# A retention layer feeding a bilinear FFN: groups 4 and 5 of the tokens go through the FFN as two blocks of 256 instead of one of 512, and one output step is placed elsewhere

## The chip, the cores and the metric

The kernel runs on one core of a Trainium2 chip. A core has a matrix engine (TensorE, PE in the profile, with its weight loads as PEld), a vector engine (VectorE, DVE), a scalar engine (ScalarE, ACT), a general engine (GpSimd, POOL), a queue that issues DMAs (SyncE, SP), and sixteen DMA engines that carry them out. Each engine works through its own list of instructions in order; the engines wait for each other through semaphores. Matmul results land in PSUM, a small memory of eight banks, and ACT or DVE must read them out before a bank can be used again.

The metric is the device time of one execution in microseconds. The time shown for a kernel is the median of its runs.

## The reference: what is computed

Eight sequences of 576 tokens, eight heads of 64 features. First a retention layer (attention without a softmax, with a decay per head), then a feed-forward block with two multiplied branches:

```python
scores = scale * np.matmul(q, k.transpose(0, 1, 3, 2))
gamma = 1.0 - 2.0 ** (-5.0 - np.arange(H, dtype=np.float32))
rel = pos[:, None] - pos[None, :]
Dmat = np.where(rel >= 0, gamma[:, None, None] ** rel[None, :, :], 0.0)
attn = np.matmul(scores * Dmat, v)              # (8, 8, 576, 64)
x = attn.transpose(0, 2, 1, 3).reshape(4608, 512)
out = ((x @ w_a) * (x @ w_b)) @ w_out           # 512 -> 1536 -> 512
```

The decay splits into a factor of the query's place and one of the key's place, so that a token's output is the sum of its own block of keys (masked scores) and a running state (the sum of key times value) over all blocks before.

## The kernel before, in words

**Groups.** The 4608 tokens are taken in 18 groups of 256, numbered from 0. Groups 0 to 2 go through an opening of their own. From group 3 on, a group is four pieces of 64 tokens, and its retention is done in small matmuls of 64x64, four of which share the array: `keyed` (L517) makes the pieces' key-value products in two PSUM tiles `kv0` and `kv1`; `matched` (L590) makes the scores of each piece with itself in `sc`; `open_outputs` (L659) starts the outputs `o` from the running states; `close_outputs` (L669) adds the masked scores times values. DVE then adds the products up to running sums (`add`, L555), ACT casts sums to states (`convert`, L567, and `convert_swapped`, L578), DVE scales outputs into the FFN's input `xT` (`scaled`, L647) and masks the scores (`masked`, L606).

**A stretch.** `stretch(into, outof)` (L679) issues these in one piece on PE: outputs of group `outof` from its states, products and scores of group `into`, outputs of `outof` from its keys. With `outof` None there are no outputs, and the products go into the PSUM buffer of `o`, which is free then; otherwise `kv0` and `kv1` are taken from the pool `ps_ffn`. `open_alone(n)` (L675) and a bare `close_outputs(n)` do a group's outputs without any scores. What DVE and ACT have to do after a stretch is put on a list, `later`, and taken off it one entry at a time by `pop` (L278) at fixed places of the FFN: the sums, the two scalings, then the first cast with the first masking, then the swapped casts with the second masking. `SPLIT` (L48) names the groups 3 and 5, whose four sums are two entries rather than one.

**The FFN.** `ffn_block` (L729) does one block of `n` tokens (`blocks`, L111: 512, 256, 256, then 512 each). For each of twelve columns F of 128 hidden features: four matmuls make `pa` (L747), ACT copies it to `ha` (L755), four make `pb` (L762), and DVE multiplies `ha` by `pb` into `hT` (L767). Each matmul streams the block's `n` tokens past a weight tile of 128x128, which is loaded for it. Then, for each 128 tokens, twelve matmuls make `po` (L781); it is copied out to `osb` by ACT (L790), or in blocks of 512 by ACT and DVE (L792) in turn, and stored by a DMA from SP. `pa`, `pb`, `po`, `kv0` and `kv1` all come from `ps_ffn`, a pool of four PSUM banks (L89). A bank can be handed on only when the reading of its tile has been issued; the choice is made when the program is built, and the new tile's first matmul waits for that reading.

**The order.** The whole order is written out by hand. The FFN's loop counts its matmuls in units of one 512-column matmul; a list `todo` (L916 to L948) holds steps with the count at which each is issued, and the FFN issues a due step at its next edge, which is the end of a `pb` or every fourth matmul of `po`. A block of 512 is 144 units (96 for `pa` and `pb`, 48 for `po`), one of 256 is 72 (48 and 24). The stretches around the change are due at 197, 240, 336, 372 and 408 units, the fifth group's outputs alone at 272 and 276. Also on the list are `ahead` (L461, POOL's casts of the loaded q, k, v), `turn` (L495, DMAs that transpose q and k into `qkT`, on SP) and `load_pair` (L140, the loads, on SP). SP issues loads, transposes and stores in the order in which the list and the FFN name them.

**The blocks and what falls in them.** Units 0 to 144 are groups 0 and 1, 144 to 216 group 2, 216 to 288 group 3, and 288 to 432 groups 4 and 5 in one block. A group's outputs must be scaled into `xT` before its block begins.

Of the kernel before, what the change touches and what calls it, by code (L numbers as in the profile page):

```python
# [18 lines left out]
def kernel(  # L19
# [15 lines left out]
    NTOK = B * S  # L35
# [72 lines left out]
    wb_sb = big.tile([128, NC, DFF], BF16)  # L108
    wo_sb = big.tile([128, NF, DM], BF16)

    blocks = [512, 256, 256] + [512] * ((NTOK - 1024) // 512)  # L111
    x_tiles = {}

    def x_of(t0, n):
# [797 lines left out]
    def turn_step(i):  # L912
# [9 lines left out]
    todo += [(136, total_of, (2,))]  # L922
    todo += [(28 + 6 * step, pair_tables, (step,)) for step in range(13)]
    todo += [(170, stretch, (3, None)), (197, stretch, (4, 3)),
             (240, stretch, (5, 4)), (272, open_alone, (5,)),
             (276, close_outputs, (5,)), (336, stretch, (6, None)),
             (372, stretch, (7, 6)), (408, stretch, (8, 7))]
    for n in range(8, NP, 2):
        todo += [(starts[n] - 116, stretch, (n + 1, n)),
# [61 lines left out]
```

## Time and profile before

| | us |
|---|---|
| median of 3 runs | 327.92 (327.43 to 328.18) |
| the profiled execution, its own time | 327.7 |
| its span, first to last instruction | 326.0 |
| PE busy | 315.8 (97%) |
| DVE busy | 161.6 (50%) |
| ACT busy | 129.5 (40%) |
| POOL busy | 116.4 (36%) |
| block of group 3, first `pa` to the next block's | 69.64 to 88.61 |
| block of groups 4 and 5 | 88.61 to 123.14 |

All durations further down are from the profiled execution; its granted clock was 1.000. A line of a timeline gives the start in us, the time until the last of the merged instructions ended, the engine, the source line, the operation with what it writes and reads, partitions and sizes, how many were merged (xN), and in brackets the idle time of the engine ahead of it with what ended that. Matmuls are pipelined: four of 256 columns are shown with 0.60 us, but the next four start 0.44 us after them. So the cost of a group of matmuls is read from start to start. A few matmul records can be missing.

### The profile page before, as it was taken

What the parts mean: (1) busy time and instruction counts of PE and PEld (TensorE: products, weight loads), DVE (VectorE), ACT (ScalarE), POOL (GpSimd) and SP (SyncE); (2) the same over time, 40 slices, a digit from 0 to 9 for tenths busy, and PEclk for the clock granted to TensorE, in tenths of its full rate; (3) what the DMA queues carried; (4) which work ended last, traced back from release to release, by engine and by line L of the source; (5) the groups of instructions that cost most, each with busy time, mean ns of one, the idle gap of its engine ahead of it and who ended that gap; (6) DMA issues with size and microseconds to landing.
All of it is one profiled execution on the core that took longest, in us unless ns stands there. A gap on an engine that the chain in (4) does not pass through costs nothing.

```text
span 326.0 us, 8627 instructions
## 1 busy us (share of the span) xinstructions
PE 315.8 (97%) x3576; PEld 165.3 (51%) x3615; DVE 161.6 (50%) x289; ACT 129.5 (40%) x286; POOL 116.4 (36%) x150
## 2 busy tenths in 40 slices
PE   8899999999999999999999999999999999999995
PEld 3564458768544554545454545454445444444443
DVE  5844454766437663845374626561556245314421
ACT  6844754453435524523253324442333233213321
POOL 3990068650867091747075205450520000000000
DMA  7999999999999989996899169925840500031013
GB/s 215 254 185 207 256 233 219 205 204 195 227 210 230 210 200 201 204 228 145 189 207 185 43 166 200 214 66 146 194 81 28 140 31 0 2 97 32 3 28 100
DMA packets 143175, 50.37 MB, mean 155 GB/s; under 512 B 124576, under 2 KB 138656, under 8 KB 143136
## 3 DMA queue, kind: packets, MB, share of 16 engines
q1 hardware_dynamic: 138384, 45.10, 66.5%
q0 software_dynamic: 4752, 4.72, 8.9%
q8 instruction: 28, 0.46, 0.6%
q14 instruction: 11, 0.09, 0.1%
HBM read 37.75 MB, written 9.44 MB: 145 GB/s over the span
## 4 chain that ended last, share of the span: by engine, by line
PE 92%; SPq 2%; DMA 2%; issue 1%; ACT 1%; DVE 1%; ACTq 0%; DVEq 0%
PE pb L762 29%; PE po L781 29%; PE pa L747 27%; SPq L159 2%; DMA qf<-in_q_dram 2%; PE o L626 2%; PE o L639 2%; PE sc L598 1%; PE kv L536 1%; PE pa L724 1%; DVE sT L350 0%; PE o L426 0%; PE sc L342 0%; PE tp L327 0%; PE tp L491 0%
## 5 line engine op out<-in xcount | busy, mean ns | idle before, releaser
L767 DVE TENSOR_TENSOR hT<-ha,pb 128x512 bf16<-128x512 bf16 (+1 forms) x120 | 75.7, 632 | 98.1 <-PE pb L762 89.9
L755 ACT CAST ha<-pa 128x512 bf16<-128x512 f32 (+1 forms) x120 | 64.7, 543 | 119.8 <-PE pa L747 115.5
L762 PE MATMUL pb<-xT,wb_sb 128*128 128x512 bf16 (+1 forms) x474 | 111.2, 358 | 0.7 <-ACT osb L790 0.2
L747 PE MATMUL pa<-xT,wa_sb 128*128 128x512 bf16 (+1 forms) x452 | 106.8, 356 | 1.4 <-issue 1.0
L781 PE MATMUL po<-wo_sb,hT 128*128 128x512 bf16 (+2 forms) x429 | 94.8, 373 | 1.7 <-issue 1.4
L762 PEld LDWEIGHTS <-wb_sb 128*128 128x128 bf16 x480 | 46.9, 98 | 47.0 <-issue 0.7
L747 PEld LDWEIGHTS <-wa_sb 128*128 128x128 bf16 x468 | 44.9, 98 | 44.3 <-issue 0.2
L781 PEld LDWEIGHTS <-hT 128*128 128x128 bf16 x444 | 41.8, 98 | 47.2
L468 POOL CAST qkb<-qf 64x1024 bf16<-64x1024 f32 x15 | 15.5, 1030 | 74.0 <-DMA qf<-in_q_dram 74.0
L473 POOL TENSOR_TENSOR vb<-vf,vs 128x1024 bf16<-128x1024 f32 x15 | 28.5, 1901 | 11.9 <-DMA vf<-in_v_dram 7.3
L792 DVE COPY osb<-po 128x512 f32<-128x512 f32 (+1 forms) x16 | 10.9, 682 | 39.7 <-PE po L781 39.7
L790 ACT COPY osb<-po 128x512 f32<-128x512 f32 (+1 forms) x21 | 12.0, 570 | 45.2 <-PE po L781 44.7
L649 DVE TENSOR_TENSOR xT<-o,qs 128x512 bf16<-128x512 f32 x30 | 19.5, 682 | 5.2 <-PE o L639 5.2
L468 POOL CAST qkb<-kf 64x1024 bf16<-64x1024 f32 x15 | 15.7, 1047 | 12.3 <-DMA kf<-in_k_dram 11.7
L561 DVE TENSOR_TENSOR sums<-kv,sums 128x256 f32<-128x256 f32 x44 | 18.6, 423 | 2.8 <-PE kv L536 0.8
L607 DVE TENSOR_TENSOR sT<-sc,mask 128x512 bf16<-128x512 f32 x30 | 19.5, 679 | 0.0
L472 POOL CAST qkb<-kf 64x512 bf16<-64x512 f32 x30 | 17.6, 614 | 0.9
L472 POOL CAST qkb<-qf 64x512 bf16<-64x512 f32 x30 | 17.6, 614 | 0.6
L565 ACT CAST states<-sums 64x512 bf16<-64x512 f32 x26 | 16.0, 616 | 0.3
L310 POOL CAST qkb<-kf 128x512 bf16<-128x512 f32 x5 | 3.1, 614 | 16.5 <-DMA kf<-in_k_dram 16.5
L666 ACT COPY fence<-o 128x2 f32<-128x2 f32 x15 | 2.4, 161 | 16.2 <-PE o L626 16.2
L350 DVE TENSOR_TENSOR sT<-sc,mask_s 128x1024 bf16<-128x1024 f32 x6 | 7.3, 1221 | 2.5 <-PE sc L342 2.5
(87 smaller groups left out, 163.0 us busy)
## 6 DMA issues: line engine op xcount, KB each, us to landing
qf<-in_q_dram SPq DMA_DIRECT2D x32, 256.0 KB, 4.8
kf<-in_k_dram SPq DMA_DIRECT2D x32, 256.0 KB, 5.1
vf<-in_v_dram SPq DMA_DIRECT2D x32, 256.0 KB, 5.1
out_dram<-osb SPq DMA_DIRECT2D x25, 256.0 KB, 2.3
out_dram<-osb SPq DMA_DIRECT2D x20, 128.0 KB, 2.7
wo_sb<-in_moe_w_out_dram POOLq DMA_DIRECT2D x3, 512.0 KB, 16.0
qf<-in_q_dram SPq DMA_DIRECT2D x8, 128.0 KB, 3.3
kf<-in_k_dram SPq DMA_DIRECT2D x8, 128.0 KB, 3.4
```

Of the source, the lines that this page charges most:

```text
L468: nc.gpsimd.tensor_copy(qkb[0:64, w], t[0:64])
L472: nc.gpsimd.tensor_copy(to[:, :, 1 - r], fro[:, :, r])
L473: nc.gpsimd.tensor_tensor(vb.rearrange("p (k h d) -> p k h d", k=2, h=H), vf.rearrange("p (k h d) -> p k h d", k=2, h=H), vs2[:, 2 if n in ...
L561: nc.vector.tensor_tensor(sums[:, i], own, prev, op=ALU.add)
L565: nc.scalar.copy(to(half(1 - r)), fro(half(r)))
L607: nc.vector.tensor_tensor(sT[:, on].rearrange("p c k s -> p (c k) s"), sc[:, on].rearrange("p c k s -> p (c k) s"), mask3.unsqueeze(1).to_ ...
L649: nc.vector.tensor_tensor(x_of(t0, 128).rearrange("p c (a s) -> p c a s", a=2), o[:, :, :, kp].rearrange("p a c s -> p c a s"), qs[:, :, s ...
L747: nc.tensor.matmul(pa[:, 0:n], wa_sb[:, c, fs], xT[:, c], start=(c == 0), stop=(c == NC - 1))
L755: nc.scalar.copy(ha[:, 0:n], pa[:, 0:n])
L762: nc.tensor.matmul(pb[:, 0:n], wb_sb[:, c, fs], xT[:, c], start=(c == 0), stop=(c == NC - 1))
L767: nc.vector.tensor_tensor(hT[:, F, 0:n], has[F][:, 0:n], pb[:, 0:n], op=ALU.mult)
L781: nc.tensor.matmul(po[:, 0:width], hT[:, F, u * 128:(u + 1) * 128], wo_sb[:, F, cols], start=(F == 0), stop=(F == NF - 1))
```

## The change

The block of groups 4 and 5 becomes two blocks of 256. So group 5's outputs are needed 72 units later, at 360 instead of 288: its outputs alone (at 272 and 276) go away, and the stretch at 336, which had only group 6's products and scores, now has group 5's outputs as well. The stretch of group 5's scores with group 4's outputs moves from 240 to 256 units.

```diff
-    blocks = [512, 256, 256] + [512] * ((NTOK - 1024) // 512)
+    blocks = [512] + [256] * 4 + [512] * ((NTOK - 1536) // 512)
...
     todo += [(170, stretch, (3, None)), (197, stretch, (4, 3)),
-             (240, stretch, (5, 4)), (272, open_alone, (5,)),
-             (276, close_outputs, (5,)), (336, stretch, (6, None)),
+             (256, stretch, (5, 4)), (336, stretch, (6, 5)),
              (372, stretch, (7, 6)), (408, stretch, (8, 7))]
```

All other due times stay. In units, the two new blocks are 288 to 360 and 360 to 432, and everything from 432 on is the same list of steps as before.

## The prediction

> **What bounds the kernel now.** I read the page's busy times and its chain of waits first, then the timelines of PE, ACT and DVE from 64 to 124 us, since the change touches nothing before the block of group 3 and nothing after 432 units.
>
> From the page:
>
> ```profile
> span 326.0 us, 8627 instructions
> ...
> PE 315.8 (97%) x3576; PEld 165.3 (51%) x3615; DVE 161.6 (50%) x289; ACT 129.5 (40%) x286; POOL 116.4 (36%) x150
> ...
> PE 92%; SPq 2%; DMA 2%; issue 1%; ACT 1%; DVE 1%; ACTq 0%; DVEq 0%
> ```
>
> PE is the bound: it works 97% of the span and carries 92% of the chain. ACT and DVE are half idle as a mean, but the chain has 1% of each, and that 1% is all in the 256 blocks. PE's timeline in the block of group 3:
>
> ```profile
> 71.34 0.60 PE L762 MATMUL pb<-xT,wb_sb 128*128 128x256 bf16 x4 [0.23 <-ACT osb L790]
> ...
> 72.64 0.60 PE L747 MATMUL pa<-xT,wa_sb 128*128 128x256 bf16 x4
> 73.08 0.60 PE L762 MATMUL pb<-xT,wb_sb 128*128 128x256 bf16 x4
> 73.52 0.60 PE L747 MATMUL pa<-xT,wa_sb 128*128 128x256 bf16 x4
> ...
> 76.61 0.61 PE L747 MATMUL pa<-xT,wa_sb 128*128 128x256 bf16 x4
> 77.06 0.60 PE L762 MATMUL pb<-xT,wb_sb 128*128 128x256 bf16 x4
> 77.68 0.60 PE L747 MATMUL pa<-xT,wa_sb 128*128 128x256 bf16 x4
> 78.24 0.60 PE L762 MATMUL pb<-xT,wb_sb 128*128 128x256 bf16 x4
> 78.74 0.60 PE L747 MATMUL pa<-xT,wa_sb 128*128 128x256 bf16 x4
> 79.42 0.60 PE L762 MATMUL pb<-xT,wb_sb 128*128 128x256 bf16 x4
> 79.85 0.60 PE L747 MATMUL pa<-xT,wa_sb 128*128 128x256 bf16 x4
> ```
>
> Undisturbed, a `pa` or `pb` of 256 columns takes 0.44 us from start to start (72.64, 73.08, 73.52), 109.4 ns a matmul. After the stretch that ends at 76.61 the starts are 0.45, 0.62, 0.56, 0.50, 0.68, 0.43 apart: three columns take 3.24 us instead of 2.625, a stall of 0.615 us. The reason is the banks: `kv0` and `kv1` hold two of four until DVE has added them up, so each `pa` waits for ACT's copy of the last, each `pb` for DVE's product. DVE in the same stretch:
>
> ```profile
> 77.76 0.42 DVE L767 TENSOR_TENSOR hT<-ha,pb 128x256 bf16<-128x256 bf16 x1 [1.81 <-PE pb L762]
> 78.10 0.42 DVE L561 TENSOR_TENSOR sums<-kv,own 128x256 f32<-128x256 f32 x1
> 78.55 0.42 DVE L561 TENSOR_TENSOR sums<-kv,sums 128x256 f32<-128x256 f32 x1
> 78.94 0.42 DVE L767 TENSOR_TENSOR hT<-ha,pb 128x256 bf16<-128x256 bf16 x1
> ```
>
> Here group 5 is one of the two whose sums are split, so only two (0.45 us apart) stand ahead of the next product. ACT before the stall of 71.34:
>
> ```profile
> 67.86 0.41 ACT L568 CAST states<-sums 128x256 bf16<-128x256 f32 x1
> 68.27 1.24 ACT L565 CAST states<-sums 64x512 bf16<-64x512 f32 x2
> 69.53 0.82 ACT L565 CAST left_states<-sums 64x256 bf16<-64x256 f32 x2
> 70.70 0.58 ACT L790 COPY osb<-po 128x512 f32<-128x512 f32 x1 [0.35 <-PE pb L762]
> ```
>
> An odd batch's second half has four swapped casts, 2.06 us of ACT in a row; in a `po` phase they cost PE 0.39 us (71.34 instead of 70.95). In blocks of 512 a column lasts 1.73 us, and there is no such stall: 96 + 48 matmuls of 216 ns (93.80 to 95.52 is eight) are 31.1 us, and with the stretches below that is the block's 34.5 us to 0.03.
>
> **The change part by part**, on PE unless another engine is named.
>
> (1) *Half the columns per matmul.* In `pa` and `pb` 96 matmuls of 512 become 192 of 256: 192 x 109.4 ns = 21.00 against 96 x 216 = 20.74. **+0.26 us.** `po` stays at 48 matmuls of 512.
>
> The Trainium skill ("TensorE: Matmul & The Clock Gate", section "Back-to-back issue gap") speaks harder against the change: in a real stream of weight loads and matmuls it gives some 81 ns a matmul at 128 columns and 131 at 512. Read straight between them, 256 would take 98 ns (an estimate from that page), two of them 65 ns more than one of 512, and this step would cost 6.2 us. The rows above, 109.4 and 216, decide: the page's 131 is not met anywhere in this trace.
>
> (2) *Stretches put together.* A full stretch costs 1.33 us: the `pb` started at 107.49 would hand over at 108.355, and the next `pa` starts at 109.69 (its `pb` at 110.55 less four matmuls). Group 6's stretch without outputs: 98.975 to 99.71, 0.735. Group 5's outputs alone: the `po` phase from 82.47 to 88.61 lasts 6.14 less 24 x 216 ns, 0.96. So 0.96 + 0.735 go and 1.33 comes. **-0.36 us.** The stretch lands on the last `pb`, so a `po` phase of 5.2 us follows: DVE's four sums (1.8), scalings (1.3) and masks (1.3) fit, ACT's two plain casts (0.8) and two swapped (1.24) end just before the second `osb` copy. No stall taken; without that cover it would be the 0.39 of (4) in the block of group 3.
>
> (3) *Group 5's scores at 256 instead of 240 units.* Two columns follow instead of three. Of the 0.615 us, the first five starts remain (0.18 + 0.12 + 0.06, the fifth tile now being `po`); the sixth, 0.24, goes. 0.615 - 0.37: **-0.24 us.**
>
> (4) *Group 7's scores at 372 units.* They fell into a block of 512 without a stall; now they fall behind the third column of a block of 256, with all that makes stalls there: group 7 is not split, and it is an odd batch's second half. With T for the start of the next `pa`, and the lags of the timeline above: `pa` T, T+1.07, T+2.13; `pb` T+0.45, T+1.63; DVE's first product at T+1.15, then all four sums at T+1.49 to T+3.26. The third `pb` gets `kv0`'s bank, free after the third sum at T+2.81, and starts at T+2.86 instead of T+2.19: 0.67 us. DVE then gives products 0.94 us apart (80.12, 81.06, 81.99 before) against PE's 0.875; one `pb` is 0.09 late. Then ACT: `ha` of column 7 is done at about T+5.2, the four swapped casts fill ACT until T+7.2, `ha` of column 8 until T+7.6. In the order of the built kernel, `pa` of column 10 reuses the bank of column 8's: it can start at T+7.67 instead of T+6.89, 0.78. Together **+1.54 us**. Below, nothing (if casts and sums are hidden as in the 512 blocks); above, 0.67 plus all 2.06 of ACT, 2.7. I take the middle, because the same queues in the block of group 3 gave 0.615 and 0.39.
>
> (5) *ACT and DVE work.* 24 `ha` of 373 ns replace 12 of 585 (ACT +1.9 us), 24 products of 418 replace 12 of 686 (DVE +1.8), two `osb` copies go from DVE (690) to ACT (586). Hidden under PE except where (4) counts them.
>
> (6) *SP and POOL.* The order of SP is unchanged up to group 7's transposes; then one store of the new block stands ahead of group 8's. Group 7's were issued at 101.0 and 103.2 and the second landed 3.8 us later, at 107.0; SP issues without a break before them, so they do not come earlier. Group 7's scores were at 109.0; now block 2 (of group 3) ends at 69.64 + 15.68 + 0.39 + 1.33 + 0.37 = 87.4, block 3 at 104.4, and the stretch starts at 107.05, its scores 0.65 later at 107.7. Margin 0.7 us: 0 taken, up to +1 if SP is slower. The added store waits for an `osb` of about 103.3, when SP still issues transposes, and takes 0.4 to 0.8; group 8's transposes land near 111, its scores come at 118. POOL's values of group 8 now wait for group 5's outputs at 99, and POOL needed them at 104: nothing.
>
> Sum: 0.26 - 0.36 - 0.24 + 1.54 = **+1.2 us**. The profiled execution took 327.7, 0.2 under the median; it would be 328.9, and the median 327.92 + 1.2 = 329.1. Everything from 432 units on moves by the same amount.
>
> **The rivals.**
>
> *R1, not slower: the four banks cover ACT's burst.* The mechanism is (4)'s last term: after column 7 PE can run two columns ahead (1.75 us) if both products have been made. If so the 0.78 goes, and the sum is +0.42; with the sums hidden too (as if `kv0` and `kv1` came free early) it is 0.26 - 0.36 - 0.24 = -0.34. It decides where ACT's hold-up stays under about 1.3 us; against it stands its length, 2.06. 327.6 to 328.4.
>
> *R2, group 7's transposes land late.* SP's transposes took 1.25 to 2.6 us to issue and 3.1 to 5.2 to land; 1 or 2 us more than above and PE stands in front of the scores, 0.3 to 1.3 us, on top of (4). Against it: the order ahead is unchanged and SP does not wait for PE there. 329.4 to 330.4.
>
> *R3, the stall at 372 feeds itself.* A late `pb` delays DVE, whose masks delay the scores of group 8 at 408 (one `sc` buffer), and ACT's late `ha` reaches into that stretch, whose outputs wait for ACT's fence copy. Up to the 2.7 of (4): 330.3.
>
> **How the numbers follow.** 0.2% of 328 is 0.66 us, about what a measurement of this kernel can tell from no change. My case, +0.7 to +1.9: 0.60. R2, to +2.5: 0.10. R3, +1.9 to +2.7: 0.08. R1: 0.22, of which 0.18 within 0.2% and 0.04 below. Slower is 0.78. The range leaves out R1's lower half and the top of R2 and R3: 328.2 to 330.5.
>
> **What would show it.** Right: from 69.64 to the block at 432 units 54.7 us instead of 53.5; `pa` and `pb` of 256 at 0.44 us in the new blocks; one piece of 1.33 us at the end of the first new block and none before it; behind group 7's stretch a `pa` that waits 0.6 to 0.9 us for ACT `ha`, and a weight load or `pb` that waits for DVE `sums`. Wrong: these waits under 0.5 us in all (R1), a wait of PE `sc` for the DMA of `qkT` (R2), waits at the stretch of group 8 (R3), or a difference that arises after 124 us, of which nothing here tells.

## The result, and the profile after

The median went from 328.05 us (327.43 to 329.16, six runs) to 329.59 us (329.38 to 330.74, six runs). The ratio is 1.0051, with a 95% interval of 1.0038 to 1.0064: the change makes the kernel slower by half a per cent, 1.5 us. The profiled execution took 329.72 us, its span is 328.0, its mean granted clock 0.998.

From the page of the changed kernel:

```profile
span 328.0 us, 8900 instructions
...
PE 319.9 (98%) x3711; PEld 174.7 (53%) x3711; DVE 162.3 (49%) x299; ACT 132.4 (40%) x300; POOL 116.6 (36%) x150
...
q8 instruction: 29, 0.48, 0.6%
...
PE 92%; SPq 2%; DMA 2%; ACT 1%; DVE 1%; issue 1%; ACTq 0%; DVEq 0%
...
L747 PE MATMUL pa<-xT,wa_sb 128*128 128x512 bf16 (+1 forms) x516 | 110.9, 340 | 0.9 <-ACT ha L755 0.9
```

PE's share of the span rose from 97% to 98% and its busy time by 4.1 us. The busy time alone would mislead. The trace of the kernel before lacks records, 3576 matmuls against 3615 weight loads, and shows fifteen idle gaps of 0.16 us that end with "issue", 2.4 us in all; the trace of the changed kernel has 3711 of each and no such gap. And a group of four matmuls is drawn 0.16 us longer than the step to the next one, so every wait is drawn that much too short. What is to be read is the length of the blocks, from the first `pa` of one to the first `pa` of the next:

| from, to | before | after |
|---|---|---|
| opening, up to the block of group 3 | 69.64 | 70.24 |
| block of group 3 | 18.98 | 17.47 |
| of it, waiting for `osb` | 0.39 | 0.08 |
| blocks of groups 4 and 5 | 34.52 | 17.02 + 20.41 |
| from 432 units to the end | 202.86 | 202.88 |

Lengths are worked out from unrounded starts and can differ by 0.01 from those of the printed ones. After 432 units nothing changed, to 0.02 us. The 0.60 us of the opening arose before any edit, and the wait for `osb` differs from execution to execution where the code is the same (0 to 2.2 us in the table below; 2.15 us of ACT's idle time there end with the landing of a store in e10). Without these two, the block of group 3 lost 1.21 us and the new blocks cost 2.91: +1.70 us in the profile, against +1.54 in the medians and +1.2 in the prediction.

The block of group 4 has nothing in it but its matmuls and one full stretch: 96 x 109.4 ns + 24 x 216 ns + 1.33 = 17.02 us, and it lasts 17.02. The block of group 5 has two full stretches, so it should last 18.35. It lasts 20.41, and the 2.07 us over lie in the stretch of group 7 (0.11) and behind it. PE's timeline there:

```profile
108.79 0.61 PE L747 MATMUL pa<-xT,wa_sb 128*128 128x256 bf16 x4
109.23 0.60 PE L762 MATMUL pb<-xT,wb_sb 128*128 128x256 bf16 x4
110.04 0.61 PE L747 MATMUL pa<-xT,wa_sb 128*128 128x256 bf16 x4 [0.20 <-ACT ha L755]
110.78 0.60 PE L762 MATMUL pb<-xT,wb_sb 128*128 128x256 bf16 x4
111.22 0.60 PE L747 MATMUL pa<-xT,wa_sb 128*128 128x256 bf16 x4
112.04 0.61 PE L762 MATMUL pb<-xT,wb_sb 128*128 128x256 bf16 x4 [0.22 <-DVE sums L561]
112.49 0.60 PE L747 MATMUL pa<-xT,wa_sb 128*128 128x256 bf16 x4
...
115.61 0.60 PE L762 MATMUL pb<-xT,wb_sb 128*128 128x256 bf16 x4
116.85 0.60 PE L747 MATMUL pa<-xT,wa_sb 128*128 128x256 bf16 x4 [0.65 <-ACT ha L755]
```

An undisturbed group starts 0.44 us after the one before. From 108.79 to 112.49 there are six steps from start to start, 2.62 us in all if nothing waited, and they take 3.70: 1.07 us of stall. Then 1.24 us pass between 115.61 and 116.85, a stall of 0.80, with 0.07 more just ahead of it. The brackets name only 0.20, 0.22 and 0.65: the idle time that the view shows is less than what is lost, because the four overlapping matmuls of a group are drawn 0.60 us long. DVE and ACT at the same place:

```profile
107.61 0.42 DVE L767 TENSOR_TENSOR hT<-ha,pb 128x256 bf16<-128x256 bf16 x1 [0.45 <-ACT ha L755]
110.31 0.42 DVE L767 TENSOR_TENSOR hT<-ha,pb 128x256 bf16<-128x256 bf16 x1 [2.28 <-PE pb L762]
110.65 1.79 DVE L561 TENSOR_TENSOR sums<-kv,sums 128x256 f32<-128x256 f32 x4
```

```profile
114.45 1.25 ACT L565 CAST states<-sums 64x512 bf16<-64x512 f32 x2
115.72 0.82 ACT L565 CAST left_states<-sums 64x256 bf16<-64x256 f32 x2
116.44 0.63 ACT L755 CAST ha<-pa 128x256 bf16<-128x256 f32 x2
```

DVE's first product behind the stretch starts 1.52 us after the first `pa` (110.31 - 108.79), where the prediction had 1.15, and the four sums follow it. The third `pb` (112.04) waits for the third sum. ACT's four swapped casts run from 114.45 to 116.54, and the `pa` of 116.85 waits for the copy of a column that is queued behind them.

### The profile page after: what moved, and what is told of

Its sections match the earlier page's. It is cut to its first block, busy times and chain, and to the rows that moved or that the text cites. A ratio compares the mean times of both kernels' runs of the same rounds, so it can differ in the third digit from the quotient of the medians.

```text
span 328.0 us, 8900 instructions
## 1 busy us (share of the span) xinstructions
PE 319.9 (98%) x3711; PEld 174.7 (53%) x3711; DVE 162.3 (49%) x299; ACT 132.4 (40%) x300; POOL 116.6 (36%) x150
## 4 chain that ended last, share of the span: by engine, by line
PE 92%; SPq 2%; DMA 2%; ACT 1%; DVE 1%; issue 1%; ACTq 0%; DVEq 0%
PE po L781 29%; PE pb L762 28%; PE pa L747 28%; SPq L159 2%; DMA qf<-in_q_dram 2%; PE o L626 2%; PE o L639 1%; PE sc L598 1%; PE kv L536 1%; PE pa L724 1%; DVE sT L350 0%; DVE sums L561 0%; PE o L426 0%; ACT states L565 0%; PE sc L342 0%
## 5 line engine op out<-in xcount | busy, mean ns | idle before, releaser
L767 DVE TENSOR_TENSOR hT<-ha,pb 128x512 bf16<-128x512 bf16 (+1 forms) x132 | 77.6, 590 | 104.5 <-PE pb L762 89.0
L755 ACT CAST ha<-pa 128x512 bf16<-128x512 f32 (+1 forms) x132 | 66.6, 508 | 118.0 <-PE pa L747 115.4
L762 PE MATMUL pb<-xT,wb_sb 128*128 128x512 bf16 (+1 forms) x528 | 113.6, 340 | 0.4 <-DVE sums L561 0.2
L747 PE MATMUL pa<-xT,wa_sb 128*128 128x512 bf16 (+1 forms) x516 | 110.9, 340 | 0.9 <-ACT ha L755 0.9
L781 PE MATMUL po<-wo_sb,hT 128*128 128x512 bf16 (+2 forms) x444 | 97.1, 374 | 0.0
L762 PEld LDWEIGHTS <-wb_sb 128*128 128x128 bf16 x528 | 51.6, 98 | 42.7 <-DVE sums L561 0.5
L747 PEld LDWEIGHTS <-wa_sb 128*128 128x128 bf16 x516 | 49.6, 98 | 41.7 <-issue 1.5
L790 ACT COPY osb<-po 128x512 f32<-128x512 f32 (+1 forms) x23 | 13.1, 571 | 46.3 <-PE po L781 46.3
L792 DVE COPY osb<-po 128x512 f32<-128x512 f32 (+1 forms) x14 | 9.5, 682 | 36.0 <-PE po L781 36.0
L808 PE MATMUL w<-ones 128*128 128x512 bf16 x19 | 7.1, 495 | 1.5 <-DVE idxp_f L203 1.5
```

Of the source, the lines that this page charges most:

```text
L747: nc.tensor.matmul(pa[:, 0:n], wa_sb[:, c, fs], xT[:, c], start=(c == 0), stop=(c == NC - 1))
L755: nc.scalar.copy(ha[:, 0:n], pa[:, 0:n])
L762: nc.tensor.matmul(pb[:, 0:n], wb_sb[:, c, fs], xT[:, c], start=(c == 0), stop=(c == NC - 1))
L767: nc.vector.tensor_tensor(hT[:, F, 0:n], has[F][:, 0:n], pb[:, 0:n], op=ALU.mult)
L781: nc.tensor.matmul(po[:, 0:width], hT[:, F, u * 128:(u + 1) * 128], wo_sb[:, F, cols], start=(F == 0), stop=(F == NF - 1))
```

## The experiments

The experiments' own times scatter by 1 to 4 us even for the kernel before (327.1 to 331.5 in the same sessions): in their profiles the block of group 3 began anywhere from 69.5 to 72.5 us, and its wait for `osb` was 0 to 2.2 us, mostly in kernels whose edit lies behind that. So a ratio of 0.3% says little here, and the readings rest on the lengths of the blocks in the profiles, one execution of each kernel. Column "3" is the block of group 3 without its wait for `osb`; columns "4" and "5" are the two new blocks (one of 512 in the kernel before).

| kernel | 3 | 4 | 5 | sum | median, and ratio to before |
|---|---|---|---|---|---|
| before | 18.59 | 34.52 together | | 53.11 | |
| after | 17.38 | 17.02 | 20.41 | 54.81 | 329.59, 1.0051 [1.0038, 1.0064] |
| e4 new blocks only | 18.59 | 16.41 | 20.30 | 55.30 | 330.53, 1.0071 [1.0039, 1.0103] |
| e1 sums first | 17.38 | 17.02 | 19.87 | 54.27 | 329.28, 1.0041 [1.0017, 1.0065] |
| e2 casts on POOL | 17.38 | 17.02 | 20.19 | 54.59 | 330.10, 1.0056 [1.0030, 1.0083] |
| e3 both | 17.38 | 17.02 | 21.98 | 56.38 | 329.72, 1.0028 [0.9997, 1.0059] |
| e5 transposes early | 17.38 | 17.02 | 20.39 | 54.79 | 330.76, 1.0078 [1.0047, 1.0109] |
| e9 e3 and e5 | 17.38 | 17.02 | 18.95 | 53.35 | 329.42, 1.0021 [0.9988, 1.0055] |
| e10 transposes late | 17.38 | 17.02 | 22.02 | 56.42 | 334.75, 1.0217 [1.0172, 1.0262] |
| e12 PE's list moved | 17.38 | 17.02 | 20.37 | 54.77 | 331.27, 1.0090 [1.0061, 1.0120] |
| e13 e9 and e12 | 17.38 | 17.02 | 18.65 | 53.05 | 329.47, 1.0034 [1.0015, 1.0053] |
| e15 DVE's list moved | 17.38 | 17.02 | 20.01 | 54.41 | 331.39, 1.0111 [1.0083, 1.0138] |

That columns 3 and 4 agree to 0.01 us over the ten executions with the places of the changed kernel (all but before and e4) shows how well the lengths can be compared. Two kernels that mend more places come at the end.

**e4: the new blocks, with the old places of the steps.**

```diff
-             (256, stretch, (5, 4)), (336, stretch, (6, 5)),
+             (240, stretch, (5, 4)), (272, open_alone, (5,)),
+             (276, close_outputs, (5,)), (336, stretch, (6, None)),
```

> One part of the change alone: the two blocks of 256, with the old places of the steps (stretch of group 5 at 240, group 5's outputs alone at 272 and 276, group 6's stretch without outputs at 336). Nothing is left out. Theory: the merge and the later stretch were worth 0.36 and 0.24, so this is 0.6 slower than the changed kernel, 330.2 (329.9 to 330.5), 2.1 above the kernel before; group 7's stretch shows the same stalls. Rival (the merged stretch is itself what costs): it is as fast as the kernel before plus 0.3, or at least faster than the changed kernel.

The sum is 2.19 us above before and 0.49 above the changed kernel. Put apart: the block of group 3 is again as long as before, 1.21 more than after; the block of group 4 is 0.61 shorter, and 96 x 109.4 ns + 24 x 216 ns + 0.735 is 16.42, where 16.41 was measured. Together 0.60, what steps (2) and (3) of the prediction had (0.36 + 0.24). The block of group 5 is 0.11 shorter here. So the stretches and the half columns were sized right, and the miss is in step (4).

**e1: the sums of group 7 ahead of the next product.**

```diff
+        if into in (7,):
+            for _ in range(2 if into in SPLIT else 1):
+                pop()
```

> The changed kernel, with group 7's four sums issued by DVE right behind its stretch instead of behind the next column's product. Nothing is left out. Theory (two of four PSUM banks are held by the products until DVE has summed them, and DVE sits idle for 2.28 us at that place): the sums run from about 108.2 to 110.0 us, the waits of pa and pb in the first three columns after the stretch (1.06 us in the profile of the changed kernel) shrink to 0.1 to 0.3, the stall of 0.8 us behind ACT's swapped casts stays, as these are as long as before. Time 328.7 to 329.1, that is 0.5 to 0.9 below the changed kernel's 329.6. Rival (the columns after the stretch are slow for another reason: late transposes of group 7, or the instruction supply after a dense stretch): the same 329.6, with the gaps still there while the sums are done early.

The block of group 5 fell by 0.54 us. The starts behind the stretch are 108.83, 109.28, 110.31, and then regular: one stall of 0.59 instead of 1.07. The one for ACT's casts stays, 0.88. So the sums do hold the banks, but taking them out of the way gave back only half.

**e2: the two `left_states` casts of group 7 on POOL.**

```diff
-                swapped(lambda r: left_states[r, batch // 4, batch % 4],
-                        lambda r: sums[r, 3])
+                copy = nc.gpsimd.tensor_copy if n == 7 else nc.scalar.copy
+                for r in (0, 1):
+                    copy(left_states[half(1 - r), batch // 4, batch % 4],
+                         sums[half(r), 3])
```

> The changed kernel, with group 7's two casts of the last running sum (0.82 us) on POOL, which is idle there from 106.6 to 115.8, instead of ACT. Nothing is left out. Theory (pa of column 10 waits for a bank whose copy stands behind 2.06 us of swapped casts on ACT): ACT's hold-up falls to 1.25 us, which two columns of lead (1.75 us) cover nearly, so the wait of 0.8 us falls to 0 to 0.4 and the time by 0.4 to 0.8, to 328.8 to 329.2. The first three columns stay as slow as they are (1.06 us). Rival (the four banks cover the burst and the wait there has another cause): no change, 329.6.

With 0.82 of ACT's 2.07 us of swapped casts gone, the late stall fell from 0.87 to 0.47, and the block to 20.19. What is left of it on PE:

```profile
115.75 0.60 PE L749 MATMUL pa<-xT,wa_sb 128*128 128x256 bf16 x4
116.66 0.60 PE L764 MATMUL pb<-xT,wb_sb 128*128 128x256 bf16 x4 [0.31 <-ACT ha L757]
```

That cast queue is the cause of the late stall. Not all of the 0.40 came through: the stall behind the stretch was larger here (1.25 instead of 1.07), because the second `pa` came 1.75 us after the first instead of 1.25. Its releaser is given as ACT's copy of the column, which ended 0.73 us earlier.

**e3: both edits.**

> Both edits together: group 7's sums right behind its stretch, and its two last casts on POOL. Theory: nearly all of the stall behind group 7's stretch goes, 1.3 to 1.8 us, and the time is 327.8 to 328.3, what the other three terms give alone (before, 328.05, plus 0.26 for the half-width matmuls, minus 0.36 for the merged outputs, minus 0.24 for the later stretch of group 5, that is 327.7) or a little over. Rival (the two blocks of 256 cost something that has nothing to do with group 7's stretch): it stays above 328.8.

This profile fell the other way: 21.98 us. PE's timeline shows rival R2 in the flesh:

```profile
109.80 0.45 PE L600 MATMUL sc<-qkT 64*64 64x64 bf16 x32 [1.83 <-DMA qkT<-qkb]
...
110.44 0.61 PE L752 MATMUL pa<-xT,wa_sb 128*128 128x256 bf16 x4
...
111.60 1.06 PE L752 MATMUL pa<-xT,wa_sb 128*128 128x256 bf16 x4
```

One of the sixteen pieces of group 7's second transpose landed at 109.76, the others by 108.23; the scores wanted it at 107.97. In the changed kernel's profile the landing was at 107.70 and the scores at 107.95, a margin of 0.25 us (the prediction said 0.7). The stop cost more than itself, since matmuls from 111 on take twice as long. The table by stretches (PE, PEld, DVE, ACT and POOL busy, then the granted clock, the DMA share and GB/s):

```profile
110.00:111.00 1.00, 1.00 (x70) 0.90 (x57) 0.00 (x0) 0.00 (x0) 0.79 (x2) 1.00 1.13 236
111.00:112.00 1.00, 1.00 (x7) 0.72 (x5) 0.08 (x1) 0.37 (x1) 0.00 (x0) 0.51 1.37 116
...
113.00:114.00 1.00, 1.00 (x7) 0.69 (x6) 0.38 (x2) 0.07 (x1) 0.00 (x0) 0.50 1.28 248
...
115.00:116.00 1.00, 1.00 (x12) 0.90 (x10) 0.99 (x3) 0.76 (x3) 0.00 (x0) 1.00 0.98 216
```

The clock was granted at half from 111.0 to 114.4. As e3's times reach from 327.3 to 332.2, this is one execution and not the rule.

**e5: group 7's transposes early.** In the list of due times for the transposes:

```diff
-    turns = {4: 116, 5: 145, 6: 240, 7: 338, 8: 345}
+    turns = {4: 116, 5: 145, 6: 240, 7: 270, 8: 345}
```

> The changed kernel with group 7's transposes issued on SP at 270 units instead of 338, ahead of the load of group 8. In the changed kernel they were issued at 101.37 and 104.01 us and the last one landed at 107.7, while PE wanted them at 107.95. Here they should land some 5 us earlier. Theory (banks, sums and ACT's casts cost the time): the second new block, 20.42 us from its first pa to the next block's, stays between 20.2 and 20.5, and the time within 0.3 us of 329.6. Rival R2 (group 7's transposes are on the edge and cost time in many executions): the block falls to 20.1 or less, the median by 0.4 to 1.0 us, and the executions that were 1 to 2 us above the median become rare.

SP issued all four transposes of groups 6 and 7 from 91.29 to 96.74, the last of them 11 us ahead of the scores. The block of group 5 lasts 20.39, as before the edit. So R2 is not what the changed kernel paid in its profile. The times did not fall either, and did not scatter less (329.5 to 336.0).

**e9: the two edits of e3, with the transposes early.**

> The two edits of the third experiment (group 7's sums ahead of the next product, its two left_states casts on POOL) together with group 7's transposes at 270 units. In the third experiment's profile the transposes landed at 109.76 us and PE stood 1.83 us. Theory: with that gone, of the 1.06 and 0.80 us of stall behind group 7's stretch 0.4 to 0.6 and 0.0 to 0.45 are left, so the second new block lasts 19.0 to 19.7 us instead of 20.42, and the time is 0.7 to 1.4 us under the changed kernel's: 328.2 to 328.9, ratio to before 1.000 to 1.0025. If the late transposes had nothing to do with the spread of the third experiment's times (327.3 to 332.2), the spread stays and the median is again near 329.7.

The block falls to 18.95, 1.46 below the changed kernel, and within 0.24 of the kernel before in the sum. The late stall is gone. One stall of 0.56 is left, right behind the stretch:

```profile
110.97 0.61 PE L752 MATMUL pa<-xT,wa_sb 128*128 128x256 bf16 x4
111.41 0.60 PE L767 MATMUL pb<-xT,wb_sb 128*128 128x256 bf16 x4
112.41 0.61 PE L752 MATMUL pa<-xT,wa_sb 128*128 128x256 bf16 x4 [0.40 <-DVE sums L561]
```

The third sum, for which that `pa` waits, was done at 111.93, half a microsecond before it started. In e1 it was the same: sum done at 109.80, `pa` at 110.31. In both, as in e2, something else let PE go.

**e10: group 8's transposes late,** since they were taken to have landed at the time in question (109.95 to 110.11 in the changed kernel):

```diff
-    turns = {4: 116, 5: 145, 6: 240, 7: 338, 8: 345}
+    turns = {4: 116, 5: 145, 6: 240, 7: 338, 8: 376}
```

> The changed kernel with group 8's transposes at 376 units instead of 345, behind loads of 256 KB. In the changed kernel ACT, DVE and PE each started an instruction 0.2 to 0.4 us later than what they waited for around 110 us, when group 8's transposes landed (109.95 to 110.11); in two experiments the same lag moved with that landing. If the landing or issue of these transposes makes the lag, it goes here: the stall of 1.06 us behind group 7's stretch falls to 0.7, the second new block from 20.42 to 20.0, unless the transposes now come too late for group 8's scores (118.9 us), which the trace shows as a wait of sc for the DMA. If not, block and stall stay within 0.15 us.

The reading behind it was wrong: what lands from 109.95 to 110.11 in the changed kernel is the output store issued at 105.78, and group 8's transposes land by 111.00 and 112.09, after the lag. Moving them did not help either: the lag grew, and the transposes came too late for group 8's scores.

```profile
110.76 0.60 PE L762 MATMUL pb<-xT,wb_sb 128*128 128x256 bf16 x4
112.53 0.61 PE L747 MATMUL pa<-xT,wa_sb 128*128 128x256 bf16 x4 [1.17 <-issue]
...
122.56 0.45 PE L598 MATMUL sc<-qkT 64*64 64x64 bf16 x32 [0.99 <-DMA qkT<-qkb]
```

The second `pa` starts 2.21 us after the first, although ACT's copy had been done for 1.2 us, and the view gives "issue" as the reason: nothing that the profile shows. What keeps a nearly constant distance is another thing, the DMA queue of PE's instructions (q8 in the page of the changed kernel). Its packets are 16,384 bytes; 29 of them for the 7447 instructions of PE's list make 256 instructions each (64 bytes an instruction). In this execution one was read from 109.90 to 110.94, and PE went on at 112.53, 1.59 us later. In the changed kernel it was read until 108.60 and the second `pa` began at 110.04, 1.43 later; in e2 1.49, in e5 1.48, in e9 1.41, in e1 1.52. In e4 PE stopped one instruction earlier, within the `pb`:

```profile
109.51 0.90 PE L762 MATMUL pb<-xT,wb_sb 128*128 128x256 bf16 x4
110.25 0.60 PE L747 MATMUL pa<-xT,wa_sb 128*128 128x256 bf16 x4
...
112.33 0.61 PE L762 MATMUL pb<-xT,wb_sb 128*128 128x256 bf16 x4 [0.30 <-DVE sums L561]
```

The first `pb` here takes 0.74 us to the next start instead of 0.44: its fourth matmul ran at 110.14, 0.41 after the third, and the `pb` of the third sum is late all the same. And e4's list of PE has one instruction more up to here. Counted in the built kernels, it is the 3011th instruction of PE in both.

**e12: 64 more PE instructions ahead of everything,** in a place where PE waits:

```diff
-    warm(8, 512)
+    warm(40, 64)
```

> The changed kernel with 64 more PE instructions ahead of everything: the first eight warm-up matmuls of 512 columns become 40 of 64 columns, in a stretch where PE waits anyway. Nothing else changes. Theory: PE's instructions come in loads of 16 KB, 256 instructions; in the changed kernel a load boundary falls on the first weight load of the second pa behind group 7's stretch (instruction 3011 of PE's list; in the kernel with the new blocks only, whose list is one longer, on the last matmul of the pb before it, also 3011), and PE stood there until 1.3 to 1.6 us after the load's packet had been read, in all profiles so far. Shifted by 64 the boundary falls into the stretch, the load before it is done long before, and that stop is gone: the second pa starts 1.05 to 1.10 us after the first instead of 1.25. If DVE's late product (0.42 us after its semaphores) goes with it, the second new block falls from 20.4 to 20.0; if not, it stays at 20.3 to 20.4. Rival (the stop is a late semaphore of ACT): the second pa still starts 1.2 to 1.25 us after the first.

```profile
68.34 0.25 PE L639 MATMUL o<-sT,vb 64*64 64x64 bf16 x7 [0.28 <-issue]
...
110.41 0.61 PE L747 MATMUL pa<-xT,wa_sb 128*128 128x256 bf16 x4
110.86 0.60 PE L762 MATMUL pb<-xT,wb_sb 128*128 128x256 bf16 x4
111.48 0.60 PE L747 MATMUL pa<-xT,wa_sb 128*128 128x256 bf16 x4
112.41 0.60 PE L762 MATMUL pb<-xT,wb_sb 128*128 128x256 bf16 x4 [0.33 <-DVE hT L767]
```

The second `pa` now starts 1.07 us after the first, as the prediction had it. And PE stops somewhere else: in the middle of an earlier stretch, at the 26th of 32 matmuls, the 1731st instruction. 3011 - 1731 is 1280, five times 256. So PE's stop behind the stretch was a late load of instructions. A stretch is 256 PE instructions (128 matmuls, each with its weight load) in 1.3 us; a boundary near its start makes PE use up a whole load before the next one is there.

The Trainium skill ("Runtime: NRT & Kernel Launch", section "Instruction fetch mechanics") describes the same blocks of 16 KiB and 256 instructions, and calls the cost of crossing one mostly hidden. It is hidden in the FFN, where 256 instructions are 128 matmuls of at least 109.4 ns, 14 us; the stops of 0.2 to 1.2 us here show that it is not behind a dense stretch.

But the block stays at 20.37. The second and third `pb` wait for DVE as before: the product behind the stretch still begins 0.415 us after DVE's wait for its two inputs has ended, where 0.045 is usual. The kernel's time is 1.7 us above the changed kernel's; in the profile the block of group 3 begins 1.75 us later, 0.47 of it in the block where PE now stops.

**e13: e9 with the shift of e12.**

> Group 7's sums first, its two left_states casts on POOL, its transposes at 270 units, and 64 more PE instructions in the opening. Without the shift the second new block lasted 18.95 us, and the second pa behind group 7's stretch started 1.44 us after the first, at the end of the third sum and also 1.4 us after the read of an instruction load. If the sums decide, it stays at 1.40 to 1.45 and the block at 18.9 to 19.0. If the instruction load decides, the second pa starts earlier, down to 1.1 us after the first, and the block lasts 18.5 to 18.7.

```profile
109.33 0.61 PE L752 MATMUL pa<-xT,wa_sb 128*128 128x256 bf16 x4
109.78 0.60 PE L767 MATMUL pb<-xT,wb_sb 128*128 128x256 bf16 x4
110.34 0.61 PE L752 MATMUL pa<-xT,wa_sb 128*128 128x256 bf16 x4
```

1.01 us instead of 1.44, right behind the third sum (110.30), and 18.65 us for the block. The load of instructions, and not the sums, had set that start in e9.

**e15: eight more DVE instructions ahead of everything.** DVE's late product is the 193rd instruction of DVE's list in the changed kernel, e2, e5, e10 and e12, and in each it starts 0.415 us after DVE's wait for its inputs has ended, 0.37 us late. In e4 the 193rd is the first sum, one instruction later, and the product is on time.

```diff
+    pad = const.tile([128, 8], FP32)
+    for i in range(8):
+        nc.vector.memset(pad[:, i:i + 1], 0.0)
```

> The changed kernel with eight one-column memsets of a scratch tile on DVE in the opening, so that DVE's list is eight instructions longer ahead of everything else; PE's list is that of the changed kernel. In the changed kernel and four experiments with the same DVE order, the product behind group 7's stretch started 0.415 us after both its semaphores; in the kernel with the new blocks only, whose list is one instruction shorter there, the product came at once (0.066 us) and the first sum 0.07 us late. In all it is the instruction with the same number in DVE's list. Theory (a boundary between two loads of DVE's instructions, 0.41 us where no running operation covers it): here the product starts 0.07 us after its semaphores, 1.10 to 1.20 us after the first pa instead of 1.52; the third pb waits for the third sum only until 2.85 us after the first pa instead of 3.25; the second new block falls from 20.4 to 20.0 us, which is what the prediction gave within 0.1; the time falls by 0.4. Rival (the product is late for a reason that lies at this place): the product stays at 1.5 us and the block at 20.3 to 20.45.

DVE, and PE:

```profile
111.58 0.42 DVE L767 TENSOR_TENSOR hT<-ha,pb 128x256 bf16<-128x256 bf16 x1 [1.82 <-PE pb L762]
111.92 1.79 DVE L561 TENSOR_TENSOR sums<-kv,sums 128x256 f32<-128x256 f32 x4
```

```profile
110.43 0.61 PE L747 MATMUL pa<-xT,wa_sb 128*128 128x256 bf16 x4
110.88 0.60 PE L762 MATMUL pb<-xT,wb_sb 128*128 128x256 bf16 x4
111.68 0.61 PE L747 MATMUL pa<-xT,wa_sb 128*128 128x256 bf16 x4 [0.20 <-ACT ha L755]
112.13 0.60 PE L762 MATMUL pb<-xT,wb_sb 128*128 128x256 bf16 x4
112.75 0.60 PE L747 MATMUL pa<-xT,wa_sb 128*128 128x256 bf16 x4
113.31 0.61 PE L762 MATMUL pb<-xT,wb_sb 128*128 128x256 bf16 x4
```

The product starts 1.15 us after the first `pa`, the third `pb` 2.88 us after it (prediction: 1.15 and 2.86; changed kernel: 1.52 and 3.25). PE's own late load is still there, 1.25 us to the second `pa`, and costs nothing, since the next `pb` waits longer anyway. The block is 20.01 us, the prediction's 19.89 (18.35 + 1.54) within 0.12. The time of this kernel is nevertheless 331.39: its opening, where the memsets stand, took 1.45 us longer up to the block of group 3 than the changed kernel's.

**e8 and e14: mended versions.** e8 is the kernel before with group 5's sums first and all such `left_states` casts on POOL; e14 has the same in the changed kernel, with group 7's sums first too, early transposes, and the shift of e12.

> The kernel before (block of 512 for groups 4 and 5, old places of the steps) with group 5's sums issued ahead of the next product, and all left_states casts of the odd batches' second halves on POOL instead of ACT. Theory: of the stall of 0.615 us behind group 5's stretch and the 0.39 us of osb behind group 3's, 0.2 to 0.4 and 0.2 to 0.39 go: 0.3 to 0.8 us under before, ratio 0.9975 to 0.999. Rival (DVE's sums only move the wait from pb to pa; casts on POOL take longer and delay states): within 0.2 us of before.

> The same with the sums first for group 5 as well and all left_states casts of the odd batches' second halves on POOL. The block of group 3 should fall from 17.38 us (without its wait for osb) to 17.0 to 17.3, the two new blocks stay at 17.0 and 18.6 to 19.0, so from the block of group 3 to 432 units 52.8 to 53.4 us instead of 54.9 in the changed kernel and 53.5 in the one before: the time 0 to 0.7 us under before, ratio 0.998 to 1.000. Rival: POOL's casts come too late for the states and a stretch waits for them; then it is above before.

The three blocks sum to 52.76 us in e8 (18.24 and 34.52) and to 52.84 in e14 (17.17, 17.02, 18.65), against 53.11 before. In times, e8 has a median of 327.56 against 328.30, ratio 0.9997 [0.9962, 1.0032]; e14 329.60 against 328.27, ratio 1.0031 [1.0011, 1.0051], and neither is shown to beat the kernel before. The medians of e13 and e14 stay 1.2 and 1.3 us above it, when their blocks do not. In their profiles the difference lies elsewhere: up to the block of group 3 they take 0.28 and 2.86 us more than before (0.79 of the 2.86 in the block with the late load of instructions at 68 us), and their waits for `osb` are 0.57 and 0.20 longer. What sets these two stays open.

## Why the prediction was right, and where it was not

It gave 329.1 us, slower; 329.59 was measured, 0.5 us over its middle value and inside its range. Of the 0.5, 0.13 is the kernel before itself, whose median was 327.92 then and 328.05 with the later runs. By its steps:

- **(1), half the columns, +0.26.** Right: 16.41 and 17.02 us for the new block of group 4 are the sums of 109.4 and 216 ns and the stretch, to 0.01.
- **(2) and (3), stretches put together and group 5's later place, -0.60.** Right: after against e4 is 0.60 in blocks 3 and 4.
- **(4), group 7's stretch in a block of 256, +1.54.** The mechanism was right, the size not: 2.07 us. The term for banks and sums was mis-sized, 0.67 foreseen and 1.07 measured. It took the lags from the block of group 3, and so the product at 1.15 us; the product came at 1.52, because the 193rd instruction of DVE starts 0.37 us late and happens to be this product; that it fell there was bad luck, which the prediction had no term for. With that instruction elsewhere (e15) the third `pb` is where the prediction had it, to 0.02. The terms for DVE's pace and for ACT's burst were right, 0.09 and 0.78 against 0.07 and 0.80, down to the `pa` of column 10 that waits for column 8's copy; e2 and e9 show the casts to be the cause of the latter. The last 0.11 is the stretch itself, 1.44 us instead of 1.33; it was 1.33 to 1.44 in the other profiles but e3's, and what makes it vary stays open.
- **(5), hidden work.** Right: no wait outside the place of (4).
- **(6), SP and POOL at nothing.** Right in the profile and in e5; but the margin that the prediction put at 0.7 us was 0.25, and in e3 it was gone.
- **R1, the banks cover ACT's burst:** wrong, 0.87 us of stall there. **R2:** not in the changed kernel's profile; real in one execution of e3 (1.83 us, and then half the clock). **R3:** wrong; the stretch of group 8, at 118.69, shows no wait.
- One reading of the page was wrong, without weight in the sum: the 1% that ACT and DVE have of the chain is not all in the 256 blocks. Of ACT's 3.2 us 2.0 lie in the opening, of DVE's 2.8 us 1.2.

Shown are the casts, the late product and the late load, each by an edit aimed at it. That the late product has to do with a load of DVE's instructions is inferred: the shift by eight shows that it goes by the place in the list. The traces hold more for it. In all fourteen the 65th instruction of DVE's list, at 37 to 40 us, starts 0.44 to 0.46 us after the one ahead of it has ended, in e15 too, where another product stands at this place; 193 less 65 is 128. And 0.7 to 2.4 us after the start of the 65th and of the 193rd, a packet of 8,192 bytes is read on the second instruction queue (q14): 128 instructions of 64 bytes. As the read comes after the delay, it is not what DVE waited for; what takes the 0.37 us stays open.

## What to carry to other kernels

When a block gets half as wide, each piece of other engines' work in it has half the cover: list where each burst falls by columns, and price the bank that it holds, not its busy time. A burst of small matmuls is also a burst of instructions, and where a load boundary falls in it depends on the count of instructions ahead of it, so an edit far away can add or take 0.2 to 1.2 us; compare the lengths of untouched and touched blocks before a difference in the total is put down to the edit.

## What was not expected of the hardware

- PE's instructions come in loads of 256. A load took about 1 us to read, and PE went on 1.3 to 1.6 us after the read had ended. A stretch of 256 instructions in 1.3 us outruns it: stops of 0.2 (after), 0.28 (e12), 0.59 (e14) and 1.17 us (e10), given as "issue" in three of the four and as a wait for ACT's `ha` in the first, which hides what they are.
- DVE starts an instruction 0.37 us late at places of its list that are 128 apart, and it shows where nothing running covers it; in e14 it is at another product, again the 193rd instruction (0.41 us after its wait, where 0.045 is usual).
- Half the clock for over 3 us after PE had stood for 1.83 us (e3), while 2.03 us of standing at 71 us in e10 left the clock at 1.00. The Trainium skill ("TensorE: Matmul & The Clock Gate", section "Part 1: The HAM clock gate (the "warmup" mystery)") has the clock fall after an idle window of about 3.4 us; the stop in e3 was shorter than that. In the clock records here a stretch at one clock lasts a whole number of steps of 3.413 us (31, 1 and 63 of them in e3). The stop in e3 lies inside one step, 107.61 to 111.02, and PE is idle for 54% of it; the one in e10 is cut by the edge of a step at 72.09, and neither step has PE idle for more than 35%. The ends of the traces agree: in each of the thirteen with clock records the clock falls after the first step of which PE is idle for 63% or more, and no step with 45% (e14, at its end) or less is followed by a fall. So in these runs the idle share of a step decides, with the edge between 45% and 54%, and not the length of the stop.
